# Linear attention into a SwiGLU layer: batch 1's q transposed in one block of 64-row tiles, with its loads and its denominators placed earlier

## The chip, the cores and the metric

The kernel runs on one core of a Trainium2 chip. The metric is the device time of one execution in microseconds (us). The engines are TensorE (PE in the profile; its weight loads are PEld), VectorE (DVE), ScalarE (ACT), GpSimd (POOL) and SyncE (SP). GpSimd issues all input loads but two, SyncE issues the output stores, and the DMA engines carry them.

## The reference, cut to what matters

```python
# q, k, v: (8, 8, 576, 64) float32
def phi(x):
    return np.where(x > 0, x, np.exp(x) - 1.0) + 1.0
q_p, k_p = (phi(q), phi(k))
kv = np.einsum('bhsd,bhse->bhde', k_p, v)
z = np.sum(k_p, axis=2)
num = np.einsum('bhsd,bhde->bhse', q_p, kv)
den = np.einsum('bhsd,bhd->bhs', q_p, z)[..., None] + 1e-06
x = (num / den).transpose(0, 2, 1, 3).reshape(4608, 512)
# w_gate, w_val: (512, 1536); w_out: (1536, 512)
g = x @ w_gate
out = (g * (1.0 / (1.0 + np.exp(-g))) * (x @ w_val)) @ w_out
```

The first part is attention without a softmax. Each head's k and v collapse to one 64x64 matrix (kv) and one vector of 64 (z); every row of phi(q) is multiplied by both, and the quotient is x. The second part is the gated layer on 4608 rows of x.

## The kernel before, in words

**Layout.** A batch has 576 positions, cut into J = 9 columns j of 64 positions. Two halves of the heads (hh = 0, 1) fill the two halves of the 128 partitions, so the tiles `kr`, `qr`, `vr` hold [128 partitions, 4 head pairs, 9 x 64]. `lp` (0 or 1) names two of these head pairs. All products are fp16 with float32 accumulation.

**Groups.** The 72 units (batch, j) go in 9 groups of 8 units, each 512 rows of x. Group 0 is j = 0 to 7 of batch 0. Group 1 is j = 8 of batch 0 and j = 0 to 6 of batch 1. For every group, layer 1 (`l1`, L292; `l1_mm`, L276, where it is cut into chunks) multiplies x, held transposed in `xT`, by 12 blocks fb of w_gate and w_val; ScalarE makes the silu (`sil`, L120) and VectorE the product (`hT`, L285). Layer 2 (`l2_mm`, L299) multiplies `hT` by `wo` for four tiles t of 128 rows, and the results leave through `osb` (`l2_out`, L322 or L120).

**Order.** The program is written under a manual schedule: each engine executes its instructions in the order in which the code names them, and waits only for the data and buffers that an instruction needs. So the order of the calls is the order of each queue. The eight PSUM banks form four pairs, handed out in turn by `pair()`.

**Batch 0 and batches from 2 on.** Batch 0 has an opening of its own (its q arrives by two SyncE loads and is transposed on TensorE by `q_turn`). From batch 2 on, q is scaled on VectorE and transposed by DMA (`dtr`, L233), with a chain spread over layer 1 of the group before (`chain`).

**Batch 1** is prepared in a third way, inside `layer2_0()`, the layer 2 of group 0. That layer runs fb outside and t inside: for fb = 0 to FO - 1, four matmuls (t = 0 to 3), with steps of batch 1 ahead of some fb; then for each t the rest of its fb. FO is 9. The steps are:

- `s0` (at fb 1): exp of k and q on ScalarE, then phi of both on VectorE (`mx_p`, `mn_q`, `add_p` for q, L374, L155, L377; `mn_k`, `add_k` for k, L147, L159), and the small phi of column j = 8 of batch 0 (`phi_q8`, L390 to L392).
- `s1` (fb 6) and `s3` (fb 8): `turn(lp, ps)`, eight transposes of 128x128 by the identity `id16` for one lp (L370) into one PSUM bank, which ScalarE copies to `qT[1]`. `s3` also turns column 8 of both batches (`turn8`, L382; `copy8`, L385) and forms z (`p1_z`, L524, L526; `Zr`, L528).
- `s4`, behind the loop over fb: `den`, q.z for both lp (L254), whose result ScalarE takes through Ln (`lnt`) and Exp with scale -1 (`rd`), that is the reciprocal.
- ahead of t = 2: k.v (`kv_corner`, L185) and its copies `R` (L201); ahead of t = 3: the numerators (`nx`, L254) and their products with `rd` into `xT` (`xmul`, L411), from which layer 1 of group 1 starts.

q.z uses the pairs `dz` (lp 0) and `cq` (lp 1); `dz` also takes k.v and the numerator of lp 0, `cq` the turn and the numerator of lp 1.

**Loads.** GpSimd issues them in one written order (L332 to L352): after the weights of layer 1 come k of batch 1, and w_out in thirds (`ld_w2`) with the two halves of q of batch 1 between them, then v of batch 1.

Of the kernel before, what the change touches and what calls it, by code (L numbers as in the profile page):

```python
# [8 lines left out]
FP16 = mybir.dt.float16  # L9
AF = mybir.ActivationFunctionType  # L10
# [3 lines left out]
P = 128  # L14
# [3 lines left out]
def kernel(  # L18
# [10 lines left out]
    nc = tc.nc  # L29

    B, H, S, D = q.shape
# [3 lines left out]
    C = 64  # L35
    J = S // C
# [12 lines left out]
    def many(shape, dt, name, n=2):  # L49
        return [sb.tile(shape, dt, name=f"{name}_{i}") for i in range(n)]  # L50

    kr = many([P, HL, J * D], FP16, "kr", NB)
    qr = many([P, HL, J * D], FP16, "qr", NB)
    vr = many([P, HL, J * D], FP16, "vr", NB)
    ek = many([P, 2, J, 2 * D], FP16, "ek")
    eq = many([P, HL, J * D], FP16, "eq")
    kp = many([P, 2, J, 2 * D], FP16, "kp")
    qp = many([P, 2, J, 2 * D], FP16, "qp")
    qT = many([P, 2, J, 2, C], FP16, "qT")
# [22 lines left out]
    id16 = sb.tile([P, P], FP16, name="id16")  # L82
    id64 = sb.tile([P, D], FP16, name="id64")
# [18 lines left out]
    def ld(src, dst, b, lp):  # L102
        nc.gpsimd.dma_start(out=dst[b % NB][:, 2 * lp:2 * lp + 2, :],  # L103
                            in_=src[b].rearrange("(l a) (c j) d -> (a c) l (j d)", a=2, j=J)[:, 2 * lp:2 * lp + 2, :])

    def ld2(src, dst, b):
        ld(src, dst, b, 0)
        ld(src, dst, b, 1)
# [6 lines left out]
    def ld_w2(f0, f1):  # L115
        nc.gpsimd.dma_start(out=wo[:, f0:f1, :],
                            in_=moe_w_out[P * f0:P * f1, :].rearrange("(c p) f -> p c f", p=P))

    def act(out, in_, func=AF.Copy, scale=1.0, bias=0.0):
        nc.scalar.activation(out=out, in_=in_, func=func, bias=bias, scale=scale)  # L120
# [6 lines left out]
    def hs(lp):  # L127
        return slice(2 * lp, 2 * lp + 2)

    def jl(t, b, lp):  # L130
        return t[b % 2][:, lp, :, :].rearrange("p j (l d) -> p l j d", d=D)

    def lj(t, b, lp):
        return t[b % NB][:, hs(lp), :].rearrange("p l (j d) -> p l j d", d=D)

    def exp_k(b, lp):
        act(jl(ek, b, lp), lj(kr, b, lp), AF.Exp)
# [7 lines left out]
    def mn_k(b, lp):  # L145
        a = ek[b % 2][:, lp, :, :]
        nc.vector.tensor_scalar(out=a, in0=a, scalar1=1.0, scalar2=None, op0=ALU.min)  # L147
# [5 lines left out]
    def mn_q(b, lp):  # L153
        a = eq[b % 2][:, hs(lp), :]
        nc.vector.tensor_scalar(out=a, in0=a, scalar1=1.0, scalar2=None, op0=ALU.min)  # L155
# [84 lines left out]
    def units(g):  # L240
        us = [(u // J, u % J) for u in range(U * g, U * g + U)]
        res = []
        for b in sorted(set(u[0] for u in us)):
            js = [j for (bb, j) in us if bb == b]
            res.append((b, js[0], js[-1] + 1, C * us.index((b, js[0]))))
        return us, res
# [55 lines left out]
    def l2_open(g, t):  # L302
        if t % 2 == 0:
            l2p[(g, "p", t // 2)] = pair()
        l2p[(g, t)] = l2p[(g, "p", t // 2)][t % 2]
# [8 lines left out]
    def l2_out(g, t, eng, n0=0, n1=512, o=None):  # L314
        if o is None:
            o = osb[on[0] % 4]
            on[0] += 1
        ps = l2p[(g, t)]
        if eng == "A":
            act(o[:, n0:n1], ps[:, n0:n1], scale=1.0 / SC)  # L320
        else:
            nc.vector.tensor_scalar(out=o[:, n0:n1], in0=ps[:, n0:n1], scalar1=1.0 / SC, scalar2=None, op0=ALU.mult)  # L322
        for e in range(2):
            b, j = units(g)[0][2 * t + e]
            dma = nc.scalar if g == NG - 1 and t == 3 and n1 == 512 and e == 1 else nc.sync
            dma.dma_start(out=out[S * b:S * b + S, n0:n1].rearrange("(c j) f -> j c f", j=J)[j],
                              in_=o[C * e:C * e + C, n0:n1])
        return o
# [3 lines left out]
    for h in (0, 2):  # L332
        nc.sync.dma_start(out=q32[:, h:h + 2, :],
                          in_=q[0].rearrange("(l a) (c j) d -> (a c) l (j d)", a=2, j=J)[:, h:h + 2, :])
# [11 lines left out]
    ld(k, kr, 1, 1)  # L346
    ld_w2(0, 4)
    ld(q, qr, 1, 0)
    ld_w2(4, 8)
    ld(q, qr, 1, 1)  # L350
    ld_w2(8, 12)
    ld2(v, vr, 1)  # L352

# [10 lines left out]

    def turn(lp, ps):
        pt = ps[:, :].bitcast(FP16).rearrange("p (j c) -> p j c", c=P)
        for j in range(J - 1):
            nc.tensor.transpose(out=pt[:, j, :], in_=qp[1][:, lp, j, :], identity=id16[:, :])  # L370
        act(qT[1][:, lp, 0:8, :, :].rearrange("p j h c -> p (j h c)"), ps[:, :].bitcast(FP16))

    def mx_p(lp):
        nc.vector.tensor_scalar(out=jl(qp, 1, lp), in0=lj(qr, 1, lp), scalar1=0.0, scalar2=None, op0=ALU.max)  # L374

    def add_p(lp):
        nc.vector.tensor_tensor(out=jl(qp, 1, lp), in0=jl(qp, 1, lp),  # L377
                                in1=eq[1][:, hs(lp), :].rearrange("p l (j d) -> p l j d", d=D), op=ALU.add)
# [5 lines left out]
    def copy8(b, ps):  # L384
        nc.vector.tensor_copy(out=qT[b][:, :, 8, :, :].rearrange("p l h c -> p l (h c)"),  # L385
                              in_=ps[:, 256 * b:256 * b + P].bitcast(FP16).rearrange("p (l c) -> p l c", l=2))

    def phi_q8():
        r, e = qr[0][:, :, D * 8:D * 9], eq[0][:, :, D * 8:D * 9]
        nc.vector.tensor_scalar(out=r, in0=r, scalar1=0.0, scalar2=None, op0=ALU.max)  # L390
        nc.vector.tensor_scalar(out=e, in0=e, scalar1=1.0, scalar2=None, op0=ALU.min)
        nc.vector.tensor_tensor(out=qp[0][:, :, 8, :].rearrange("p a (l d) -> p a l d", d=D),  # L392
                                in0=e.rearrange("p (a l) d -> p a l d", l=2),
                                in1=r.rearrange("p (a l) d -> p a l d", l=2), op=ALU.add)
# [113 lines left out]
    def none():  # L508
        return [[] for _ in range(FB)], [[] for _ in range(4)]

    def lam(f, *a):
        return lambda: f(*a)
# [19 lines left out]
    def period0():  # L532
        sl, w = none()
        b = 1
        sl[7] = [lam(mx_k, b, 0), lam(exp_k, b, 0), lam(mn_k, b, 0), lam(add_k, b, 0)]
        sl[8] = [lam(zsum, b, 0, 1)]
        sl[10] = [lam(mx_k, b, 1)]
        return sl
# [36 lines left out]
    def layer2_0():  # L575
        for t in range(4):
            l2_open(0, t)
        p1_open()
        cq, dz = b1p["q"], b1p["z"]
        nc.scalar.preload_act_table_set("natural_log_exp_and_others")  # L580

        def den(lp, ps):
            t_corners(1, Zr, lp, ps)
            for l2 in range(2):
                act(lnt[2 * lp + l2][:, :], ps[l2][:, :], AF.Ln, bias=epsb[:, 0:1])

        def nx(lp, ps):
            t_corners(1, R, lp, ps)
            x_t(1, lp, ps)

        def s0():
            act(eq[0][:, :, D * 8:D * 9], qr[0][:, :, D * 8:D * 9], AF.Exp)
            exp_k(1, 1)
            exp_q(1, 0)
            exp_q(1, 1)
            phi_q8()
            mx_p(0)
            mn_k(1, 1)
            add_k(1, 1)
            mn_q(1, 0)  # L600
            add_p(0)
            mx_p(1)
            mn_q(1, 1)
            add_p(1)

        def s1():
            turn(0, cq[0])

        def s3():
            turn(1, cq[1])  # L610
            for b in range(2):
                for lp in range(2):
                    turn8(b, lp, dz[0])
            p1_z()
            for b in range(2):
                copy8(b, dz[0])

        def s4():
            den(0, dz)
            den(1, cq)  # L620
            for i in range(4):
                act(rd[i // 2][:, i % 2, :], lnt[i][:, :], AF.Exp, scale=-1.0)

        step = {1: [s0], 6: [s1], 8: [s3]}
        FO = 9
        for fb in range(FO):
            for f in step.get(fb, []):
                f()
            for t in range(4):
                l2_mm(0, t, fb)  # L630
        s4()
        for t in range(4):
            if t == 2:
                for lp in range(2):
                    kv_corner(1, lp, kp, True, True)
                r_copy(1, 0, 2, "VV")
            if t == 3:
                nx(0, dz)
                nx(1, cq)
            for fb in range(FO, FB):  # L640
                l2_mm(0, t, fb)
            if t < 3:
                l2_out(0, t, "V")
        exp_k(2, 0)
        exp_k(2, 1)
        l2_out(0, 3, "V")
        exp_q(2, 0)
        exp_q(2, 1)
        phi_k(2, 0)
        phi_k(2, 1)  # L650
        ring[:] = [l2p[(0, "p", 0)], dz, cq, l2p[(0, "p", 1)]]

    for g in range(NG):
        b1, b2 = g + 1, g + 2
        if g == 0:
            sl = period0()
        else:
            sl, _ = none()
# [105 lines left out]
```

## Time and profile before

| what | us |
|---|---|
| median of 4 runs | 314.59 (314.45 to 314.76) |
| the profiled execution's own time | 314.76 |
| its span (first to last instruction) | 313.0 |
| TensorE busy | 306.5 (98%) |
| VectorE busy | 204.2 (65%) |
| ScalarE busy | 153.9 (49%) |
| layer 2 of group 0 with the work in it, first L299 to the last chunked L276 | 35.8 to 53.9 |

The span is shorter than the execution by what lies around the program. A busy time counts overlapping instructions once. The chain of waits walks back from the last instruction to what released it each time; its pieces say which engine set the end at each moment. The timeline lists instructions by start and length: the end of a matmul is modelled, so the pace of matmuls is read from their starts. Times inside the span count from its start.

### The profile page before, as it was taken

Reading aid. Unit: us, or ns where it says so; the run is one execution under the profiler, and the core shown is the slowest. Engines: PE = TensorE matmul, PEld = TensorE weight load, DVE = VectorE, ACT = ScalarE, POOL = GpSimd, SP = SyncE. Lnnn points to the kernel's source line nnn. Section 1 sums busy time; section 2 is a strip of 40 time slices with the busy share of each in tenths; the row PEclk is TensorE's granted clock in tenths of the full one; section 3 lists DMA queues with packets and bytes.
Section 4 is the critical chain, followed back from the end, with each engine's and each line's share of the span. In section 5 each row is a group of like instructions: output and inputs, shape, how many; then the busy total and the mean of one; then the engine's idle time right before and its main releaser. Section 6 shows DMA issues by size and latency. Waiting matters only on the chain.

```text
span 313.0 us, 5494 instructions
## 1 busy us (share of the span) xinstructions
PE 306.5 (98%) x2169; PEld 142.5 (46%) x2169; DVE 204.2 (65%) x361; ACT 153.9 (49%) x232; POOL 47.3 (15%) x72
## 2 busy tenths in 40 slices
PE   8899999999999999999999999999999999999994
PEld 3344454444544454445444544444444444444442
DVE  4854859899699657977697859874991434143410
ACT  4955869639633745365535743475330333133311
POOL 8655334300000410032000500000000000000000
PEclk9999999999999999999999999999999999999999
DMA  8999999997512594139612990314032300140014
GB/s 217 196 197 200 206 206 237 233 207 118 118 34 41 87 188 125 38 44 179 180 33 43 126 240 0 75 41 95 2 68 58 86 1 1 40 96 0 0 36 101
DMA packets 41162, 32.80 MB, mean 105 GB/s; under 512 B 16432, under 2 KB 36144, under 8 KB 41136
## 3 DMA queue, kind: packets, MB, share of 16 engines
q0 software_dynamic: 20464, 18.29, 37.4%
q1 hardware_dynamic: 20592, 14.13, 18.8%
q8 instruction: 17, 0.28, 0.4%
q14 instruction: 9, 0.07, 0.1%
q10 hardware_dynamic: 80, 0.03, 0.0%
HBM read 37.75 MB, written 9.44 MB: 151 GB/s over the span
## 4 chain that ended last, share of the span: by engine, by line
PE 95%; DMA 2%; DVE 1%; ACT 0%; issue 0%; POOL 0%; POOLq 0%; DVEq 0%
PE pp L292 57%; PE pp L299 30%; PE pp L276 2%; DMA kr<-in_k_dram 2%; PE pp L185 2%; PE pp L254 2%; PE pp L124 0%; ACT ek L120 0%; PE pp L398 0%; PE pp L370 0%; DVE xT L411 0%; DVE kp L159 0%; PE pp L212 0%; DVE osb L322 0%; DVE ek L147 0%
## 5 line engine op out<-in xcount | busy, mean ns | idle before, releaser
L120 ACT ACTIVATE sil<-pp 128x512 f16<-128x512 f32 x108 | 63.4, 597 | 101.7 <-PE pp L292 96.6
L292 PE MATMUL pp<-xT,wg 128*128 128x512 f16 x416 | 106.8, 379 | 0.0
L292 PE MATMUL pp<-xT,wv 128*128 128x512 f16 x416 | 106.8, 379 | 0.0
L285 DVE SCALAR_TENSOR_TENSOR hT<-pp,sil 128x512 f16<-128x512 f32 x108 | 72.4, 681 | 48.9 <-PE pp L292 35.5
L299 PE MATMUL pp<-wo,hT 128*128 128x512 f16 (+2 forms) x444 | 97.1, 373 | 0.6 <-DVE osb L322 0.6
L299 PEld LDWEIGHTS <-hT 128*128 128x128 f16 x444 | 42.0, 98 | 49.8 <-issue 2.1
L292 PEld LDWEIGHTS <-wv 128*128 128x128 f16 x416 | 40.7, 98 | 49.1
L292 PEld LDWEIGHTS <-wg 128*128 128x128 f16 x416 | 40.7, 98 | 48.4
L322 DVE TENSOR_SCALAR osb<-pp 128x512 f32<-128x512 f32 (+1 forms) x19 | 12.9, 682 | 30.9 <-PE pp L299 30.9
L120 ACT ACTIVATE osb<-pp 128x512 f32<-128x512 f32 (+1 forms) x18 | 10.3, 574 | 34.8 <-PE pp L299 34.8
L120 ACT ACTIVATE ek<-kr 128x1152 f16<-128x1152 f16 x16 | 17.9, 1157 | 0.4 <-DMA kr<-in_k_dram 0.3
L120 ACT ACT_TABLE_LOAD x13 | 16.7, 1283 | 2.3 <-PE pp L292 2.1
L229 DVE TENSOR_TENSOR qp<-qp,rden 128x1152 f16<-128x1152 f16 x12 | 16.2, 1347 | 0.0
L220 DVE TENSOR_REDUCE den<-prod 128x18 f32<-128x1152 f16 x12 | 16.1, 1343 | 0.0
L120 ACT ACTIVATE eq<-qr 128x1152 f16<-128x1152 f16 (+1 forms) x15 | 15.9, 1102 | 0.1
L695 POOL COPY gate<-qT 128x1 f16<-128x1 f16 x4 | 1.0, 253 | 97.5 <-DMA qT<-qp 97.5
L271 DVE TENSOR_SCALAR xT<-pp 128x512 f16<-128x512 f32 (+1 forms) x14 | 8.8, 667 | 7.0 <-PE pp L254 7.0
L103 POOL DMA_DIRECT2D vr<-in_v_dram x16 | 11.6, 730 | 8.4 <-PE pp L292 2.6
L103 POOL DMA_DIRECT2D kr<-in_k_dram x16 | 11.5, 722 | 8.9 <-DMA vr<-in_v_dram 2.8
L159 DVE TENSOR_TENSOR kp<-ek,kp 128x1152 f16<-128x1152 f16 x16 | 12.1, 757 | 0.5
L103 POOL DMA_DIRECT2D qr<-in_q_dram x14 | 10.2, 732 | 6.8 <-DMA wo<-in_moe_w_out_dram 1.7
L147 DVE TENSOR_SCALAR ek<-ek 128x1152 f16<-128x1152 f16 x16 | 7.5, 470 | 5.7 <-ACT ek L120 5.6
(82 smaller groups left out, 180.1 us busy)
## 6 DMA issues: line engine op xcount, KB each, us to landing
out_dram<-osb SPq DMA_DIRECT2D x70, 128.0 KB, 3.5
kr<-in_k_dram POOLq DMA_DIRECT2D x16, 288.0 KB, 8.6
vr<-in_v_dram POOLq DMA_DIRECT2D x16, 288.0 KB, 9.9
qr<-in_q_dram POOLq DMA_DIRECT2D x14, 288.0 KB, 12.1
wo<-in_moe_w_out_dram POOLq DMA_DIRECT2D x3, 512.0 KB, 13.2
wg<-in_moe_w_gate_dram POOLq DMA_DIRECT2D x5, 256.0 KB, 8.5
wv<-in_moe_w_val_dram POOLq DMA_DIRECT2D x5, 256.0 KB, 9.0
q<-in_q_dram SPq DMA_DIRECT2D x2, 576.0 KB, 4.0
```

The source lines that it names most:

```text
L103: nc.gpsimd.dma_start(out=dst[b % NB][:, 2 * lp:2 * lp + 2, :], in_=src[b].rearrange("(l a) (c j) d -> (a c) l (j d)", a=2, j=J)[:, 2 * lp ...
L120: nc.scalar.activation(out=out, in_=in_, func=func, bias=bias, scale=scale)
L147: nc.vector.tensor_scalar(out=a, in0=a, scalar1=1.0, scalar2=None, op0=ALU.min)
L159: nc.vector.tensor_tensor(out=a, in0=ek[b % 2][:, lp, :, :], in1=a, op=ALU.add)
L185: nc.tensor.matmul(out=ps[hh][D * l2:D * l2 + D, D * lp:D * lp + D], lhsT=t[b % 2][rows, lp, j, D * l2:D * l2 + D], rhs=vr[b % NB][rows, 2 ...
L220: nc.vector.tensor_reduce(out=den[:, c, :], in_=prod[:, :, :].rearrange("p j (l d) -> p (j l) d", d=D), axis=AX.X, op=ALU.add)
L229: nc.vector.tensor_tensor(out=qv, in0=qv, in1=rden[:, c, :].unsqueeze(2).to_broadcast([P, 2 * J, D]), op=ALU.mult)
L271: nc.vector.tensor_scalar(out=dst, in0=ps[l2][:, c0:], scalar1=1.0 / SC, scalar2=None, op0=ALU.mult)
L285: nc.vector.scalar_tensor_tensor(out=hT[g % 2][:, fb, :], in0=ps[1][:, :], scalar=SC, in1=s[:, :], op0=ALU.mult, op1=ALU.mult)
L292: nc.tensor.matmul(out=ps[h][:, :], lhsT=w[:, c, P * fb:P * fb + P], rhs=xT[g % 2][:, c, :], start=(c == 0), stop=(c == 3))
L299: nc.tensor.matmul(out=l2p[(g, t)][:, n0:n1], lhsT=hT[g % 2][:, fb, P * t:P * t + P], rhs=wo[:, fb, n0:n1], start=(fb == 0), stop=(fb == F ...
L322: nc.vector.tensor_scalar(out=o[:, n0:n1], in0=ps[:, n0:n1], scalar1=1.0 / SC, scalar2=None, op0=ALU.mult)
```

## The change

`turn` now takes both lp and both banks of `cq` at once. It makes 32 transposes: each takes the 64 partitions of one hh, by the 64x64 identity `id64`, and writes the bank of that hh. ScalarE copies one bank to `qT[1]`, VectorE the other. The turn is one step at fb 6. The turn of column 8 and z come as `s2` at fb 7, and FO is 8, so q.z comes one fb sooner. k.v now comes ahead of t = 1, and the numerators ahead of t = 2; the output of t = 2 is copied behind the products into `xT`.

In `s0` ScalarE takes the exp of q ahead of the exp of k, and VectorE finishes q ahead of k. The exp and phi of batch 0's column 8 (`exp_q8`, `phi_q8`) are moved to layer 1 of group 0, behind fb 7 (`period0`).

Both halves of q of batch 1 are loaded ahead of the second third of w_out, which is loaded in two pieces.

```diff
@@ -346,8 +346,9 @@
     ld(k, kr, 1, 1)
     ld_w2(0, 4)
     ld(q, qr, 1, 0)
-    ld_w2(4, 8)
     ld(q, qr, 1, 1)
+    ld_w2(4, 6)
+    ld_w2(6, 8)
     ld_w2(8, 12)
     ld2(v, vr, 1)
 
@@ -364,11 +365,20 @@
 
 
 
-    def turn(lp, ps):
-        pt = ps[:, :].bitcast(FP16).rearrange("p (j c) -> p j c", c=P)
-        for j in range(J - 1):
-            nc.tensor.transpose(out=pt[:, j, :], in_=qp[1][:, lp, j, :], identity=id16[:, :])
-        act(qT[1][:, lp, 0:8, :, :].rearrange("p j h c -> p (j h c)"), ps[:, :].bitcast(FP16))
+    def turn(ps):
+        for lp in range(2):
+            for j in range(J - 1):
+                for hh in range(2):
+                    pt = ps[hh][:, :].bitcast(FP16).rearrange("p (l j c) -> p l j c", l=2, c=C)
+                    rows = slice(C * hh, C * hh + C)
+                    nc.tensor.transpose(out=pt[:, lp, j, :], in_=qp[1][rows, lp, j, :], identity=id64[rows, :])
+        for hh in range(2):
+            src = ps[hh][:, :].bitcast(FP16).rearrange("p (l j c) -> p l j c", l=2, c=C)
+            dst = qT[1][:, :, 0:8, hh, :]
+            if hh == 0:
+                act(dst, src)
+            else:
+                nc.vector.tensor_copy(out=dst, in_=src)
 
     def mx_p(lp):
         nc.vector.tensor_scalar(out=jl(qp, 1, lp), in0=lj(qr, 1, lp), scalar1=0.0, scalar2=None, op0=ALU.max)
@@ -384,6 +394,9 @@
     def copy8(b, ps):
         nc.vector.tensor_copy(out=qT[b][:, :, 8, :, :].rearrange("p l h c -> p l (h c)"),
                               in_=ps[:, 256 * b:256 * b + P].bitcast(FP16).rearrange("p (l c) -> p l c", l=2))
+
+    def exp_q8():
+        act(eq[0][:, :, D * 8:D * 9], qr[0][:, :, D * 8:D * 9], AF.Exp)
 
     def phi_q8():
         r, e = qr[0][:, :, D * 8:D * 9], eq[0][:, :, D * 8:D * 9]
@@ -532,7 +545,7 @@
     def period0():
         sl, w = none()
         b = 1
-        sl[7] = [lam(mx_k, b, 0), lam(exp_k, b, 0), lam(mn_k, b, 0), lam(add_k, b, 0)]
+        sl[7] = [lam(mx_k, b, 0), lam(exp_q8), lam(exp_k, b, 0), lam(phi_q8), lam(mn_k, b, 0), lam(add_k, b, 0)]
         sl[8] = [lam(zsum, b, 0, 1)]
         sl[10] = [lam(mx_k, b, 1)]
         return sl
@@ -589,25 +602,22 @@
             x_t(1, lp, ps)
 
         def s0():
-            act(eq[0][:, :, D * 8:D * 9], qr[0][:, :, D * 8:D * 9], AF.Exp)
-            exp_k(1, 1)
             exp_q(1, 0)
             exp_q(1, 1)
-            phi_q8()
+            exp_k(1, 1)
             mx_p(0)
+            mx_p(1)
+            mn_q(1, 0)
+            add_p(0)
+            mn_q(1, 1)
+            add_p(1)
             mn_k(1, 1)
             add_k(1, 1)
-            mn_q(1, 0)
-            add_p(0)
-            mx_p(1)
-            mn_q(1, 1)
-            add_p(1)
 
         def s1():
-            turn(0, cq[0])
-
-        def s3():
-            turn(1, cq[1])
+            turn(cq)
+
+        def s2():
             for b in range(2):
                 for lp in range(2):
                     turn8(b, lp, dz[0])
@@ -621,8 +631,8 @@
             for i in range(4):
                 act(rd[i // 2][:, i % 2, :], lnt[i][:, :], AF.Exp, scale=-1.0)
 
-        step = {1: [s0], 6: [s1], 8: [s3]}
-        FO = 9
+        step = {1: [s0], 6: [s1], 7: [s2]}
+        FO = 8
         for fb in range(FO):
             for f in step.get(fb, []):
                 f()
@@ -630,17 +640,18 @@
                 l2_mm(0, t, fb)
         s4()
         for t in range(4):
-            if t == 2:
+            if t == 1:
                 for lp in range(2):
                     kv_corner(1, lp, kp, True, True)
                 r_copy(1, 0, 2, "VV")
-            if t == 3:
+            if t == 2:
                 nx(0, dz)
                 nx(1, cq)
             for fb in range(FO, FB):
                 l2_mm(0, t, fb)
-            if t < 3:
+            if t < 2:
                 l2_out(0, t, "V")
+        l2_out(0, 2, "V")
         exp_k(2, 0)
         exp_k(2, 1)
         l2_out(0, 3, "V")
```

## The prediction

> **What bounds the kernel now.** I read the page first. Its rows of engines and of the chain that ended last:
>
> ```profile
> span 313.0 us, 5494 instructions
> PE 306.5 (98%) x2169; PEld 142.5 (46%) x2169; DVE 204.2 (65%) x361; ACT 153.9 (49%) x232; POOL 47.3 (15%) x72
> PEclk9999999999999999999999999999999999999999
> PE 95%; DMA 2%; DVE 1%; ACT 0%; issue 0%; POOL 0%; POOLq 0%; DVEq 0%
> ```
>
> TensorE is the bound: the clock is full and 95% of the chain is PE. Only PE time removed, or a PE wait removed, moves the end. The change lies in the first groups of units, so next I read the chain in order of time, there:
>
> ```profile
> 36.00 5.18 PE pp L299 x24
> 41.18 0.50 PE pp L370 x8
> 41.68 1.73 PE pp L299 x8
> 43.40 0.45 PE pp L370 x8
> 43.85 0.22 PE pp L382 x4
> ...
> 45.20 0.03 issue
> 45.23 0.64 PE pp L254 x15
> 45.86 1.40 PE pp L299 x6
> 47.26 0.73 PE pp L185 x72
> 48.00 0.75 PE pp L299 x3
> 48.75 0.62 PE pp L254 x16
> ...
> 49.39 0.69 DVE xT L411
> 50.09 0.04 issue
> 50.13 0.59 PE pp L276 x2
> ```
>
> The reader sees layer 2 of group 0 (L299, 5.18/24 = 0.216 us each) with batch 1's work between: the two turns (L370), q.z (first L254), k.v (L185), the numerators (second L254). At 49.39 the chain leaves PE: PE has run out of layer 2 and waits for the copies to xT. Last, the timeline at four places:
>
> ```profile
> 46.26 0.68 ACT L120 ACTIVATE lnt<-pp,epsb 128x512 f32<-128x512 f32 x1
> 47.19 0.80 PE L185 MATMUL pp<-vr,kp 64*64 64x64 f16 x72
> 47.93 0.39 PE L299 MATMUL pp<-wo,hT 128*128 128x512 f16 x1
> 49.25 0.82 PE L299 MATMUL pp<-wo,hT 128*128 128x512 f16 x3
> 50.34 0.38 PE L276 MATMUL pp<-xT,wv 128*128 128x512 f16 x1
> 50.73 0.38 PE L276 MATMUL pp<-xT,wg 128*128 128x512 f16 x1
> ```
>
> **The change, part by part.**
>
> *1. The wait at the seam goes: 0.39 gained.* Before, 3 layer-2 matmuls follow the numerators; the third starts at 49.69, so layer 1 could start at 49.69 + 0.216 = 49.91. It runs at full pace only from 50.73, its third matmul; counted back two steps of 0.215 that is a start at 50.30. Lost: 0.39. After, with numerators at t == 2 and FO = 8, 8 matmuls follow (1.73 us). VectorE's first copy starts 0.14 after their start (49.39 against 49.25), one copy each 0.60, the second done at +1.43: in time for +1.73. The third and fourth are done by +2.62 and wanted only at +3.45. The copies of outputs 2 and 3 now queue behind these four on VectorE; their banks are wanted by layer 1's fourth block, some 5 us later. The reciprocals (rd, ACT) keep their distance: from q.z to the numerators there are 2 matmuls fewer before k.v (-0.43), one more after it (+0.22) and the wait of point 3 (+0.23).
>
> *2. The turn: 0.22 gained.* Before: PE leaves L299 at 40.80 + 0.22 = 41.02 and is back at 41.51 (0.50); the second turn holds it from 43.24 to 43.69 (0.45). Together 0.95, at 56 ns for each of 16 transposes of 128x128. After: 32 transposes, 64 rows by 128 columns of weights with 64 moving columns, alternating between the two row halves, each half into its own bank. No row shows that form. Nearest is L185, 64x64 weights with 64 moving columns in four quadrants: 71 starts in 0.80 - 0.21 = 0.59 us, so 8.3 ns each, 33 ns for each round of the four quadrants. Two halves in step at 33 ns a round: 16 x 33 = 0.53. Entering such a mode costs (46.88 + 0.22 = 47.10 to 47.19) 0.09; leaving it (last L185 start 47.78 to 47.93) 0.15 less the 0.03 that the last round takes, 0.12. One block: 0.09 + 0.53 + 0.12 = 0.74, so 0.95 - 0.74 = 0.21, say 0.22. Bounds: 27 ns a round (half of the 56 ns of twice the columns) gives 0.43 + 0.21 = 0.64, gain 0.31; loads that take turns give 32 x 27 ns (L526, nine 128-column loads with 2 moving columns, 0.24 us) = 0.86 + 0.21 = 1.07, a loss of 0.12.
>
> Here a rule speaks against the change. The Trainium skill, "TensorEngine Tiling (Array Packing)", Instruction Overhead, says each matmul has about 60 cycles of overhead, so that one with 1 column lasts like one with 60, and warns against tiling a dimension that is already small; "TensorE: Matmul & The Clock Gate", Back-to-back issue gap, makes this about 25 ns start to start. By that 32 transposes need 0.80 + 0.21 = 1.01 and the turn loses 0.06. The trace differs where the array is tiled: 8.3 ns at L185. I take the row, and keep the rule's end in the range.
>
> *3. A new wait before k.v: 0.23 lost.* k.v accumulates into the pair that q.z of lp 0 was in, so its matmuls wait for the two Ln (lnt) that read that pair. Before, q.z starts at 45.23 and the second Ln ends at 46.26 + 0.68 = 46.94, 1.71 later; with about 0.05 for the signal (the copy of qT ends at 45.17, q.z starts at 45.23) k.v may write the second bank from 1.76. Before, 6 matmuls stand between and k.v starts at 47.19, 1.96 after q.z: hidden. After, at t == 1 with FO = 8, 4 stand between: 1.96 - 0.43 = 1.53. PE waits 1.76 - 1.53 = 0.23 at k.v's second matmul, and all of layer 2 behind it in order waits too. Nothing covers it. That ACT gets to the first Ln as soon after q.z as before holds: its copy of the turn ends about 42.9.
>
> *4. Loads.* Before, GpSimd's issues and landings (issue plus time to landing, asked of one tile at a time): first q 35.7, w_out's second third 25.03 + 13.2 = 38.2, second q 26.83 + 12.8 = 39.7, last third 42.3, v 43.7 and 45.1. One q takes 1.4 of the stream, a third of w_out 2.6. After: second q 37.1, w_out 4:6 about 38.4, 6:8 about 39.7, and from 42.3 on as before. One issue more (0.7 us of GpSimd, which sits 10 us ahead of its landings) delays nothing unless the stream loses time on a further piece; then some 0.1. Wanted: fb 4 at 35.83 + 16 x 0.216 = 39.3 (0.9 spare), fb 6 at 41.7, fb 8 at 44.6, v's second half in k.v about 46.2 (it has 1.1). The turn frees PE earlier and its cover is thus thinner, but whole. SP's queue has nothing new: output stores go out up to 1.7 us sooner, beside loads of batch 2 that ACT wants from 48.8 on and which landed from 46.5 on.
>
> *5. The order on ACT and VectorE: nothing.* The small exp and phi of q's last column (0.42 ACT, 0.23 + 0.22 + 0.29 VectorE) move into layer 1 of group 0, fb 7. There they push the next silu and the sums by about 0.32; hT of fb 9 was done at 35.75 and would be at 36.07, its bank is wanted by t = 3 at 36.48. If that cover were gone, PE would wait by the excess. In layer 2, ACT does q's exps at 37.1 and 38.1 (before 38.5), the second when q is 1 us old. VectorE: both max, then min and add for lp 0 (done 39.5), for lp 1 (done 40.7), then k (done 41.9). The turn is wanted at 41.1: no wait (before, PE had 0.04 there). k's add is wanted by q.z's sums at 42.6.
>
> *6. Copies of the turn.* Before two on ACT (1.02 each). After one on ACT, one on VectorE, side by side. VectorE's: L385 moved 256 columns in 0.28, L322's 512 of f32 0.69; 1024 columns take about 0.7 at L385's pace, up to 1.2. It starts at 41.9 and ends by 42.6 to 43.1; next in VectorE's queue is Zr, whose input is ready at 43.2. So hidden at both ends. Then Zr, two copies, q.z as before, under the 4 matmuls of fb 7 in place of fb 8: the same 0.03 of issue.
>
> *Sum:* 0.39 + 0.22 - 0.23 = 0.38 gained, in the span and carried whole to the end, since the chain after is PE without a wait. The profiled execution took 314.76 (313.0 span, 1.76 around it), the median of the four runs is 314.59: I set the 0.38 against the median, 314.2. A measurement of this kernel can tell about 0.2% (0.63 us) from no change; 0.38 is 0.12%.
>
> **The rivals.**
>
> *B, faster.* The wait of point 3 is mostly hidden, because q.z ends sooner for the Ln or the switch of modes takes longer than before: 0.39 + 0.22 = 0.61; with 27 ns rounds 0.70: 313.9. For it: only 0.23 of distance decides. Against: lnt to lnt is 0.57 in the trace, and both counts of matmuls are fixed.
>
> *C, the halves share the load path.* 32 x 27 ns: 0.39 - 0.12 - 0.23 = 0.04, 314.55. For it: the rule above. Against: L185.
>
> *D, slower.* Each 64-row transpose is as dear as a 128-row one, 56 ns as at L370, none beside another: 32 x 56 = 1.79 + 0.21 = 2.00 in place of 0.95, so -1.05 + 0.39 - 0.23 = -0.89, 315.5. It decides from the pace: above 28 ns a transpose the change loses, above 48 ns by more than 0.63. For it: no row has 128-column loads in row halves. Against: L185's quadrants overlap both loads and matmuls.
>
> *The change does nothing here:* if VectorE's copies don't follow the earlier numerators, the seam stays; then -0.01, inside C's place.
>
> **How the numbers follow.** Likeliest case 0.58 (314.2; its own range 313.95 to 314.45), B 0.20, C and the seam staying 0.12, D 0.10. Faster by over 0.2%: B, 0.20; slower: D, 0.10; within: 0.70. The range 313.7 to 315.0 leaves out D and the lower edge of B.
>
> **What would show it.** The L374 block from first start to the next L299: 0.65 right, over 1.0 wrong. Layer 1 of group 1 (L276) at 0.215 from its first matmul, no xT in the chain. An ACT lnt in the chain or a gap of about 0.2 at L185's second matmul: point 3. q.z's start at about 44.1 against 45.23. Wrong altogether if PE waits for wo at fb 4, for vr in k.v, or for qp before the turn.

## The result, and the profile after

The changed kernel takes 314.06 us (median of 33 runs, 313.75 to 314.5) against 314.54 for the kernel before (53 runs). The ratio is 0.9984, with a 95% interval of 0.9979 to 0.9989: 0.50 us faster (0.35 to 0.66), 0.16%. The forecast was 314.2, and 0.38 faster.

The page of the changed kernel shows the same bound. Its span is 0.8 shorter, and TensorE is busy for the same 98% of it:

```profile
span 312.2 us, 5524 instructions
PE 306.2 (98%) x2185; PEld 142.4 (46%) x2185; DVE 205.3 (66%) x362; ACT 152.8 (49%) x231; POOL 48.7 (16%) x73
PE 95%; DMA 2%; DVE 1%; ACT 0%; issue 0%; POOL 0%; POOLq 0%
```

The chain in order of time, over the changed stretch (start, length, engine and line; L374 is the turn, L392 to L539 column 8 and z, the L254 q.z and the numerators, L185 k.v):

```profile
35.87 5.18 PE pp L299 x24
41.05 0.57 PE pp L374 x32
41.62 0.97 PE pp L299 x4
42.59 0.22 PE pp L392 x4
...
43.95 0.03 issue
43.97 0.64 PE pp L254 x15
44.61 0.97 PE pp L299 x4
45.58 0.14 PE pp L185
45.72 0.01 issue
45.73 0.79 PE pp L185 x71
46.52 0.97 PE pp L299 x4
47.49 0.57 PE pp L254 x16
48.06 1.83 PE pp L299 x8
49.89 3.45 PE pp L276 x16
```

Three things are to be seen. There is one block of turns where there were two. Layer 1 of group 1 follows layer 2 with no copy to xT between them. And L185 now comes in two pieces, one matmul and then 71. Between them TensorE waited to be released: this is the new wait.

The traces are compared by one number: the time from the first L299 to the first L292 of group 1, both read as starts in the timeline. It is 17.91 before and 17.47 after, 0.44 less. What lies around this stretch shows no effect of the change. From the first L292 of group 0 to the first L299 it is 17.27 in all ten traces of this study, so the exp and phi of column 8, which the change moved into that part, cost nothing there. From the end of the stretch to the last L299 it is 255.43 to 255.59. The first L299 itself comes anywhere from 35.49 to 35.92, since the opening waits for its first loads. The spans of the two profiles differ by 0.8: 0.44 is the stretch, the start (35.83 before, 35.71 after) and the rest (255.59 and 255.47) give 0.12 each, and what follows the last L299 gives 0.08. Such differences come and go between runs of one kernel: the second profile of the changed kernel has its first L299 at 35.80.

### The profile page after: what moved, and what is told of

Same layout as the page of the kernel before. It is cut to its first block, busy times and chain, and to the rows that moved or that the text cites. A ratio compares the mean times of both kernels' runs of the same rounds, so it can differ in the third digit from the quotient of the medians.

```text
span 312.2 us, 5524 instructions
## 1 busy us (share of the span) xinstructions
PE 306.2 (98%) x2185; PEld 142.4 (46%) x2185; DVE 205.3 (66%) x362; ACT 152.8 (49%) x231; POOL 48.7 (16%) x73
## 4 chain that ended last, share of the span: by engine, by line
PE 95%; DMA 2%; DVE 1%; ACT 0%; issue 0%; POOL 0%; POOLq 0%
PE pp L292 58%; PE pp L299 30%; PE pp L276 2%; DMA kr<-in_k_dram 2%; PE pp L185 2%; PE pp L254 2%; PE pp L124 0%; ACT ek L120 0%; PE pp L411 0%; DVE kp L159 0%; PE pp L212 0%; PE pp L374 0%; DVE osb L322 0%; DVE ek L147 0%; DVE R L201 0%
## 5 line engine op out<-in xcount | busy, mean ns | idle before, releaser
L292 PE MATMUL pp<-xT,wv 128*128 128x512 f16 x416 | 106.8, 379 | 0.0
L292 PE MATMUL pp<-xT,wg 128*128 128x512 f16 x416 | 106.8, 379 | 0.0
L299 PE MATMUL pp<-wo,hT 128*128 128x512 f16 (+2 forms) x444 | 97.1, 373 | 0.6 <-DVE osb L322 0.6
L299 PEld LDWEIGHTS <-hT 128*128 128x128 f16 x444 | 42.0, 98 | 49.8 <-issue 2.1
L292 PEld LDWEIGHTS <-wv 128*128 128x128 f16 x416 | 40.7, 98 | 49.1
L292 PEld LDWEIGHTS <-wg 128*128 128x128 f16 x416 | 40.7, 98 | 48.5
```

The costliest lines, as they stand in the source:

```text
L292: nc.tensor.matmul(out=ps[h][:, :], lhsT=w[:, c, P * fb:P * fb + P], rhs=xT[g % 2][:, c, :], start=(c == 0), stop=(c == 3))
L299: nc.tensor.matmul(out=l2p[(g, t)][:, n0:n1], lhsT=hT[g % 2][:, fb, P * t:P * t + P], rhs=wo[:, fb, n0:n1], start=(fb == 0), stop=(fb == F ...
```

## The experiments

All eight ran beside the kernel before. Their edits are shown against the changed kernel and shortened; comments in them were added for the reader. In the table, "against changed" is the difference of the stretch from 17.47.

| run | stretch, us | against changed | ratio of times to before, 95% interval |
|---|---|---|---|
| changed kernel again | 17.47 | 0.00 | 0.9988, 0.9978 to 0.9998 |
| turn of 128x128 tiles | 17.69 | +0.22 | 0.9991, 0.9983 to 0.9999 |
| numerators late | 17.89 | +0.42 | 0.9999, 0.9990 to 1.0007 |
| k.v later | 17.26 | -0.21 | 0.9981, 0.9975 to 0.9988 |
| loads as before | 18.78 | +1.31 | 1.0026, 1.0017 to 1.0034 |
| k.v sooner | 17.90 | +0.43 | 0.9991, 0.9982 to 1.0000 |
| w_out's second third in one piece | 18.11 | +0.64 | 0.9998, 0.9990 to 1.0006 |
| column 8 of batch 0 back in s0 | 17.66 | +0.19 | 0.9989, 0.9982 to 0.9996 |

The intervals of the times reach 0.2 to 0.3 us to either side. So for differences of 0.2 the evidence is the trace; the times only do not contradict it.

**The control.** It is the changed kernel, without an edit.

> The changed kernel again, as the control on this chip. Theory (three terms on TensorE: the wait at the seam gone +0.39, the turn's block shorter +0.28 as the trace after shows it, a new wait before k.v -0.23): 0.44 faster than before, ratio 0.9986. Rival (the gain is drift ahead of the changed stretch, where the two traces already differ by 0.13): 0.3 faster, with the stretch from the first L299 to the last L276 no shorter than before.

The stretch was 17.47 again, to the hundredth, and the time 0.9988 of that before. Drift ahead of the stretch, which the stretch leaves out, is not the cause.

**The turn of 128x128 tiles.**

```diff
-    def turn(ps):                       # 2 x 8 x 2 transposes of 64 rows
+    def turn(ps):
+        for lp in range(2):
+            pt = ps[lp][:, :].bitcast(FP16).rearrange("p (j c) -> p j c", c=P)
+            for j in range(J - 1):
+                nc.tensor.transpose(out=pt[:, j, :], in_=qp[1][:, lp, j, :], identity=id16[:, :])
```

ScalarE and VectorE then copy one lp each, in place of one half each.

> The changed kernel with its one block of turns made of 16 transposes of 128x128 by the full identity, one bank for each lp; all else as changed. Theory: the block goes from 0.67 (L299 to L299) to 16 x 0.056 = 0.90 with no switch of modes, so 0.23 slower than the changed kernel, and the rest stays: 0.2 faster than before. Rival (the form of the transposes is off the path, only the earlier places count): as the changed kernel within 0.05. Rival (the small tiles cost more than they save): faster than the changed kernel.

The timeline of TensorE, first of the changed kernel, then of this one, where the turn is L372 (start, time covered, engine, line and names, shapes, count):

```profile
40.46 0.59 PE L299 MATMUL pp<-wo,hT 128*128 128x512 f16 x2
40.98 0.64 PE L374 MATMUL pp<-id,qp 64*128 64x64 f16 x32
41.56 0.39 PE L299 MATMUL pp<-wo,hT 128*128 128x512 f16 x1
```

```profile
40.47 0.59 PE L299 MATMUL pp<-wo,hT 128*128 128x512 f16 x2
40.90 1.06 PE L372 MATMUL pp<-id,qp 128*128 128x128 f16 x16
41.79 0.59 PE L299 MATMUL pp<-wo,hT 128*128 128x512 f16 x2
```

In the changed kernel the last L299 ahead starts at 40.46 + 0.216 = 40.67 and is through at 40.89. The block ends when L299 comes back at 41.56: 0.67. With full tiles it is 40.90 to 41.79, 0.89. That difference of 0.22 is the difference of the stretch. So the form of the tiles is worth 0.22, and both rivals fall.

The two blocks of before had taken 0.95, 0.05 more than this one. That is not what a second block costs. The first block of before came late, because its weights are q, which VectorE finished at 40.24 + 0.76 = 41.00, about when TensorE was through with L299 (41.01):

```profile
40.24 0.76 DVE L377 TENSOR_TENSOR qp<-qp,eq 128x1152 f16<-128x1152 f16 x1
41.05 0.45 PEld L370 LDWEIGHTS <-qp 128*128 128x128 f16 x8 [0.37 <-DVE qp L377]
```

Its first transpose started at 41.06, 0.04 late, and the next 0.01 behind the pace; the second block of before took 0.45 for its 8 transposes, half of 0.89. The 0.05 is thus this small wait, which is gone because q is ready sooner (lp 1's at 40.77). No run separates which of the earlier places of q did that.

**Numerators late.**

```diff
-            if t == 2:                  # 8 of the 16 matmuls ahead, 8 behind
+                if i == 14:             # i = 4 * t + fb - FO: 14 ahead, 2 behind
                     nx(0, dz)
                     nx(1, cq)
```

k.v stays where it is in the changed kernel, and the output of t = 2 is copied ahead of the products again.

> The changed kernel with batch 1's numerators put off until only 2 layer-2 matmuls follow them (14 of the 16 ahead), and output 2 copied ahead of the products into xT, as before. Theory: layer 1 of group 1 waits for the copies to xT again; PE comes after 0.44 us and the second copy is there about 1.24 after the numerators, so about 0.37 is lost against the changed kernel, and L276 starts with gaps. Rival (the seam was covered by something else): no gap in L276, time as the changed kernel.

The chain of this kernel leaves TensorE at the seam again, as before the change:

```profile
48.76 0.46 PE pp L254 x12
49.22 0.69 DVE xT L424
49.91 0.04 issue
49.95 0.59 PE pp L276 x2
```

It lost 0.42 (0.37 expected), and the time was that of the kernel before (0.9999). So the seam is a term of its own, and without it nearly the whole gain of 0.44 is gone.

**k.v later.**

```diff
-            if t == 1:
+                if i == 6:
                     kv_corner(1, lp, kp, True, True), lp = 0, 1
                     r_copy(1, 0, 2, "VV")
-            if t == 2:
+                if i == 10:
                     nx(0, dz)
                     nx(1, cq)
```

> The changed kernel with k.v behind 6 layer-2 matmuls after q.z instead of 4, and the numerators behind 10 instead of 8, so that 6 follow them. Theory: the two Ln are done by 1.76 after q.z's start and k.v comes at 1.96, so the wait of 0.23 goes, and the seam stays closed (second copy at +1.43, wanted at +1.30 + 0.43): 0.23 faster than the changed kernel, 0.67 faster than before. Rival (the wait only moves, to the copies R or to xT): as the changed kernel, with a gap at L254 or L276 in place of the one at L185.

Its chain, over the same part:

```profile
44.18 0.64 PE pp L254 x16
44.82 1.40 PE pp L299 x6
46.22 0.73 PE pp L185 x72
46.95 0.97 PE pp L299 x4
47.92 0.57 PE pp L254 x16
48.49 1.40 PE pp L299 x6
49.89 3.45 PE pp L276 x16
```

L185 is one piece of 72, and 0.73 long as before the change (in the changed kernel 0.14 + 0.01 + 0.79 = 0.94). No gap opens further on. The stretch is 0.21 shorter than in the changed kernel. At 0.9981 this is the fastest kernel of the study: faster than the one before, and by the trace 0.21 ahead of the changed one. The times alone do not separate it from the changed one.

**k.v sooner.** The same edit with `i == 2` for k.v and `i == 8` for the numerators, which is where the changed kernel has them.

> The changed kernel with k.v behind 2 layer-2 matmuls after q.z instead of 4, numerators where they are. Theory (k.v waits for the second Ln, 1.76 after q.z's start): the wait grows from 0.23 by the two matmuls, 0.43, to 0.66, so 0.43 slower than the changed kernel and about as before. Rival (the gap at L185 is the switch to small tiles, or v's landing): the gap stays at 0.23, time as the changed kernel.

```profile
44.03 0.47 PE pp L254 x8
44.50 1.25 ACT lnt L120 x2
45.75 0.04 issue
45.80 0.79 PE pp L185 x71
```

Here the chain itself leaves TensorE for the two Ln, and k.v's second piece starts 45.80 - 44.03 = 1.77 after q.z: the same distance as in the changed kernel (45.73 - 43.97 = 1.76). The loss was 0.43, two matmuls. A switch to small tiles would have cost the same at either place, and with k.v later the same switch showed no gap, so it is out as the cause.

This run alone doesn't rule out that k.v waits for v to land, for its second piece also starts at nearly the same time in the span as in the changed kernel (45.80 and 45.73). The run with the loads as before, further down, does. There q.z came later and v sooner (its halves landed at 43.4 and 44.9):

```profile
46.66 0.14 PE pp L185
46.81 0.01 issue
46.82 0.79 PE pp L185 x71
```

The second piece starts 2 us behind v's last landing, but again 1.76 behind q.z (45.06) and 0.05 behind the end of the second Ln (46.77). So the wait is fixed by the Ln.

**Loads as before.**

```diff
     ld(q, qr, 1, 0)
+    ld_w2(4, 8)
     ld(q, qr, 1, 1)
-    ld_w2(4, 6)
-    ld_w2(6, 8)
```

> The changed kernel with the order of loads of before (first q, w_out's second third whole, second q). Theory (the load order carries nothing by itself but holds the early turn up): the second q lands at about 40.0 instead of 37.4, VectorE's second max stands in front of everything for q, and lp 1's add ends near 43.0 instead of 40.77; TensorE waits in the turn for about 1.8, with nothing of layer 2 to go past it. So 1.8 slower than the changed kernel, 1.3 slower than before. Rival (the early turn has slack enough): as the changed kernel, landings later but no gap on TensorE.

```profile
26.61 12.83 DMA qr<-in_q_dram
39.44 0.02 issue
39.47 0.46 DVE qp L383
39.93 0.38 DVE eq L155
40.30 0.02 issue
40.33 0.76 DVE qp L386
...
42.31 0.41 PE pp L373 x16
```

The chain runs from the second half of q through VectorE's whole work on q (L383, L155, L386) to the second half of the turn (L373), as expected. The size was off: 1.31 and not 1.8. This q landed 39.44 - 35.49 = 3.95 after the first L299. I had taken it at 40.0, and 4.3 after. That is 0.3 of the difference; the rest is VectorE, which needed 2.8 from the landing to the end of its last add (42.25), where I had allowed 3.0. Whether the new load order would bring anything by itself, no run shows; without it the changed kernel is slower than the one before.

**w_out's second third in one piece.**

```diff
     ld(q, qr, 1, 1)
-    ld_w2(4, 6)
-    ld_w2(6, 8)
+    ld_w2(4, 8)
```

> The changed kernel with both q loads ahead of w_out's second third, but that third in one piece. Theory: it lands at about 40.05, where its last piece lands now, and fb 4 wants it at 39.2, so TensorE waits about 0.9 at fb 4; all behind it is that much later: 0.8 to 0.9 slower than the changed kernel, 0.4 slower than before. Rival (cover enough, the two pieces buy nothing): as the changed kernel.

```profile
39.80 0.59 PE L299 MATMUL pp<-wo,hT 128*128 128x512 f16 x2 [0.47 <-DMA wo<-in_moe_w_out_dram]
```

fb 4 starts at 39.80, where 35.71 + 16 x 0.216 = 39.17 was its turn: 0.63 late, and 0.64 lost in the stretch. Again the landing (39.76) was 0.3 earlier than expected, and the loss smaller by as much.

**Column 8 of batch 0 back in s0.**

```diff
-        sl[7] = [lam(mx_k, b, 0), lam(exp_q8), lam(exp_k, b, 0), lam(phi_q8), ...
+        sl[7] = [lam(mx_k, b, 0), lam(exp_k, b, 0), ...
         def s0():
+            exp_q8()
             exp_q(1, 0)
             exp_q(1, 1)
             exp_k(1, 1)
+            phi_q8()
```

> The changed kernel with the exp and phi of batch 0's column 8 back in front of batch 1's q (in s0), on ScalarE and VectorE. Theory: VectorE gets to q's max about 0.6 later, lp 1's add ends at about 41.35 instead of 40.77, and TensorE wants it at 41.2: 0.1 to 0.2 slower than the changed kernel, with a short gap inside the turn. Rival (hidden wholly): as the changed kernel; its L299 ahead of the turn the same, the block of turns 0.67 long.

```profile
41.25 0.34 PE pp L374 x16
41.60 0.41 PE pp L374 x16
```

The turn breaks in two: its second half waits for VectorE, whose add for lp 1 ends at 41.55, and 0.19 is lost. In the changed kernel that add ends at 40.77, 0.21 ahead of the turn, which waits for nothing.

## Why the prediction was right

**The seam** was put at 0.39. In the changed kernel the first L276 starts 0.216 after the last L299 and all 16 follow at that pace, so the whole 0.39 is gone. Putting the numerators late (2 matmuls behind them, where the kernel before has 3) costs 0.42. VectorE's copies to xT start 0.15 after the L299 that follow the numerators (48.14 against 47.99), as the prediction had it (0.14), and now 1.73 of matmuls stands over them.

**The turn** was put at 0.22 and is 0.95 - 0.67 = 0.28. The term that was mis-sized is the round of two halves: 33 ns, taken from L185's four quadrants. Measured from first to last start it is (0.64 - 0.19) / 15.5, about 29 ns, close to the lower bound of 27. So 16 rounds took 0.46 and not 0.53. The edges were right: 40.89 to 40.98 is 0.09 to enter, and about 0.1 is left for leaving. Of the 0.28, 0.05 is the wait for VectorE that the kernel before had at its first turn. The prediction had seen it (0.04, in its point 5) and counted it in the 0.95, though it put the order on VectorE at nothing.

The rule weighed against the row (the Trainium skill, "TensorE: Matmul & The Clock Gate", Back-to-back issue gap, about 25 ns from start to start) would have made 32 transposes last 0.80 or more. They lasted 0.46, on average 14.5 ns each, so here the measurement decides. Taken for each row half by itself, which began a transpose every 29 ns, the rule is not broken.

**The wait before k.v** was put at 0.23. This is the timeline of the changed kernel for the second Ln on ScalarE, and for TensorE at k.v:

```profile
45.00 0.68 ACT L120 ACTIVATE lnt<-pp,epsb 128x512 f32<-128x512 f32 x1
```

```profile
45.51 0.21 PE L185 MATMUL pp<-vr,kp 64*64 64x64 f16 x1
```

The first k.v matmul starts at 45.51 and the second at 45.73, 0.05 after the Ln has ended (45.68): 0.22 of gap. Rival B, that this wait would hide, is out.

**Loads, order and copies** were put at nothing, with their covers named. In the changed kernel the two q land at 36.0 and 37.4, the pieces of w_out at 38.7 and 40.0, v at 44.0 and 45.4. That is some 0.3 later than the prediction had it, and within the spares that it gave, though at fb 4, which starts at 39.16, the spare was 0.45 and not 0.9. lp 1's add ends at 40.77 (40.7 predicted). VectorE's copy of the turn took 0.68 and ends at 42.71, ahead of Zr at 43.10:

```profile
42.03 0.68 DVE L381 COPY qT<-pp 128x1024 f16<-128x1024 f16 x1
43.10 0.42 DVE L541 TENSOR_SCALAR Zr<-pp 128x256 f16<-128x256 f32 x1 [0.39 <-PE pp L539]
```

**The sum** of the measured terms is 0.39 + 0.28 - 0.22 = 0.45. The stretch has 0.44, and both lie in the interval of the times (0.35 to 0.66). Rival C falls with the 0.67 of the block (it needed 1.07), and D with it (2.00). That the seam stays falls with the chain, which has no copy to xT any more. The three runs that took away a support show what the covers were worth: 1.31 (loads), 0.64 (w_out's pieces) and 0.19 (column 8).

## What to carry to other kernels

When TensorE is the bound and two stages are joined by copies on another engine, count what is left to do behind the step that feeds these copies. The earlier that step, the more work stands over them; but each step moved ahead comes closer to what frees its buffer, so count that distance too (here 1.76 from q.z to the freed pair; k.v two matmuls too early cost 0.22, over half of what the seam brought). The best of the places tried was in the middle of an output tile, where both distances are kept, and not at a boundary of a loop.

## What the runs showed that I had not expected

Transposes of 64 rows by 128 columns, alternating between the two row halves, ran at 14.5 ns each on average. A round of two takes 29 ns, less than the 33 ns of a round of four 64x64 quadrants. What sets either pace, no run shows.

Landings of the same load, in the same order of loads, differ by over half a microsecond between runs (the second q of the changed order landed at 36.9 to 37.6, the last piece of w_out's second third at 39.5 to 40.1), and the start of layer 2 by 0.4. So a cover of 0.9 us for a load is less than it looks.
